# An attention and mixture-of-experts kernel: the row traffic of the expert tiles is issued in another order

## The chip, the cores and the metric

The kernel runs on one core of one Trainium2 chip. The metric is the device time of one execution in microseconds (us). Before the change three executions took 2145.89, 2147.29 and 2153.76 us; the median is 2147.29 us. A further execution, taken with the hardware profiler, is the one whose rows are read below.

## The reference, cut to what matters

```python
B, S, D, d_qk = 8, 2496, 256, 64           # attention
scores = (1 / S) * z @ z.T                 # per batch
x = u * (maximum(scores, 0) ** 2 @ v)      # [B*S, D], N = B*S = 19968 rows

E, F = 8, 1024                             # mixture of experts, one expert a row
logits = x @ w_gate + modality_bias[modality_id]
e_idx  = argmax(logits)                    # the row's expert
gate   = softmax(logits)[e_idx]
out[row] = gate * (maximum(x[row] @ w1[e_idx], 0) @ w2[e_idx])
```

All tensors are float32. Which rows go to which expert is known only when the logits of the last batch are there, so the rows of an expert have to be collected on the chip.

## The kernel before

The first part, some 1240 us, computes the attention of the eight batches, stores each row of x in `row_store` (DRAM) and, batch by batch, routes the rows: a row of `table` (DRAM) is written for each token, at a place that depends on its expert, with the gate's weight, the token's number and the row's place in `row_store`. Nothing of the change lies in its order of work; that is written out by a planner (`pieces`).

The second part runs expert tiles of 512 rows, t = -4 to 35. Tiles -4 to -1 (`EARLY` = 4) hold rows of the expert that had the most rows after seven batches; their rows lie ready when the part begins, and they run while the last batch is still being routed and the other tiles are planned. Tiles 0 to 34 are planned tiles (`UNC` = 35), tile 35 a small one; further ones (`MAXT` = 42) stand behind a branch.

A tile's work on TensorE (`run_tile`) is eight `up` products (f = 0 to 7: six matmuls each) in two groups of four. Behind each group come the `down` products of that group: 16 matmuls with the high parts `hh`, then 8 with the low parts `hl`. ScalarE makes `hh` and VectorE makes `hl` of each `up` product. All engines carry out their instructions in the order in which the program issues them, each engine its own; a DMA is issued by SyncE (SP), or by GpSimd (POOL) where rows are gathered or scattered by an index, and such an issue waits, with all that is queued behind it on that engine, until its data and its buffer are ready.

What is not TensorE's is put into slots. `aside(f)` (L1539) is called at ten places of a tile, f = 0 to 9: behind `up` 0, 1, the whole group and its `down`, the same for the second group (4, 5, 6, 7), and at the end (8, 9). It issues first what lies in the list `put_off` with a slot of at most f, then the next tile's weight quarter number f - 2 (`part_weights_high` on ScalarE, `part_weights_low` on VectorE), then what `between` holds for that slot in the four early tiles, and last the turning of the next tile's rows (`turn_blocks`, `part_high`, `part_low`; slots 5 and 6, in tiles -4 and -3 slots 3 and 4, in the few tiles without `stage` others). In the lines `put(slot, ...)` slots count on through the early tiles: 0 to 7 are tile -4, 8 to 15 tile -3, 16 to 23 tile -2, 24 to 31 tile -1.

The steps that the change moves, each with the engine that issues it:

- `scatter` (L713, POOL): writes 128 tokens' rows of `table`; twelve of them are left for the last batch.
- `plan` (L752, VectorE, five pieces): what each tile holds. Its last piece issues two DMAs on SP: `places` to DRAM, and `meta` from there back to one partition, which waits for the first to land.
- `find(t)` (L859, SP): reads the tile's place from `meta` into a register and loads its rows of `table` as `gate`. The first one waits for all scatters.
- `gather(t)` (L870, POOL): four indirect DMAs that fetch the 512 rows into `got`, by the indices that `find` loaded.
- `keep(t)` (L885, SP): stores `got` to DRAM (`picked`), and waits for the gather to land.
- `fetch(t)` (L892, SP): four DMAs that load `picked` in another arrangement, as `xg`; they wait for the store to land.
- `fetch_weights(t)` (L913, SP): four loads of 512 KB, the expert's weights. They take four of the seven buffers of the tag `x`; `got` takes a fifth.

A tile's result leaves through SP and POOL too. `send(t)` (L1441) at the tile's end: VectorE turns it (`squared`), SP stores it to DRAM (`stage`, four DMAs), in slot 2 of the next tile SP loads it back (`bring`, the tensor `back`), and in slots 4, 5, 6 and 6 ScalarE multiplies a quarter of it by the gate and POOL scatters it to `out` (`put`; in eleven of the tiles as eight DMAs in place of four). ScalarE waits in its own order for `back`, and the `hh` of the second group stand behind that wait. Tiles -2, 33 and 34 have no `stage`; their rows are scattered at once.

In a planned tile t the steps stand in this order before the change, with the slot:

```python
(2) bring of tile t-1, keep(t + 2)
(3) fetch(t + 2), find(t + 3), fetch_weights(t + 2)
(4, 5, 6, 6) put of tile t-1
(7) gather(t + 3)
```

Of the kernel before, what the change touches and what calls it, by code (L numbers as in the profile page):

```python
# [9 lines left out]
F32 = mybir.dt.float32  # L10
# [6 lines left out]
P = 128  # L17
# [5 lines left out]
def ins_of(x):  # L23
    return getattr(x, "ins", x)
# [3 lines left out]
def tile_attention_moe(ctx: ExitStack, tc: tile.TileContext, ut, v, zt, mid, wg, mb, w1, w2, out):  # L28
# [12 lines left out]
    B, S, D = v.shape  # L41
# [5 lines left out]
    J = T // P  # L47
# [5 lines left out]
    XW = 3  # L53
    BLK = 32
    CAP = N
    EARLY = min(4, (B - 1) * S // E // T)
    UNC = -(-N // T) - EARLY
    MAXT = (N + E * (T - 1)) // T - EARLY
# [26 lines left out]
    nq = const.tile([1, 1], I32, name="nq")  # L85
    first = const.tile([1, 2], I32, name="first")
    small = ctx.enter_context(tc.tile_pool(name="small", bufs=1))
    small.tile([P, 16], F32, name="room")


    ph1, feed = ExitStack(), ExitStack()
# [41 lines left out]
    n = NCOL - J  # L133
# [579 lines left out]
    def scatter(b, k):  # L713

        n = 64 if k == NCOL - 1 else P
        i = ins_of(
            nc.gpsimd.indirect_dma_start(  # L717
                out=table,
                out_offset=bass.IndirectOffsetOnAxis(ap=RT[b]["sloti"][:n, k:k + 1], axis=0),
                in_=RT[b]["side"][:n, k, :],  # L720
                in_offset=None,
                bounds_check=E * CAP - 1,
                oob_is_err=False,
            )
        )
        tc.declare_no_dep(i, group="table", reason="each token has a row of its own")
        tc.add_to_no_dep_group("table", i)
        scatters.append(i)
# [23 lines left out]
    def plan():  # L752
# [36 lines left out]
        for n, (x, op, at_least) in enumerate(((is_last, ALU.is_gt, UNC), (least, ALU.is_equal, UNC + 1))):  # L789
            k = odd[:, n:n + 1]  # L790
# [39 lines left out]
        nc.vector.tensor_copy(out=placei, in_=place)  # L830

        nc.sync.dma_start(out=places, in_=placei[0:MAXT])
        nc.sync.dma_start(out=meta, in_=places.rearrange("(o m) n -> o m n", o=1))


# [9 lines left out]
    def wait_rows(i, n):  # L845
        assert len(scatters) >= n
        for s in scatters[ready["n"]:n]:
            tc.add_manual_dep(i, s.name, data, reason="rows of tokens")
        ready["n"] = n
# [4 lines left out]
    SIDE, GOT, KEPT = {}, {}, {}  # L854

    def order_of_rows(t):
        return "(p j) c -> p j c" if is_staged(t) else "(j p) c -> p j c"

    def find(t, r0=0, nj=J):  # L859

        cell = first[0:1, 1:2] if t < 0 else meta[0:1, t, 0:1]
        row = nc.sync.value_load(cell, min_val=0, max_val=(E - 1) * CAP if t < 0 else E * CAP - T)
        side = small.tile([P, J, XW], F32, tag="gate", bufs=6, name="gate")[:, 0:nj, :]
        r0 += (t + EARLY) * T if t < 0 else 0
        src = table[bass.ds(row + r0 if r0 else row, nj * P), :]
        i = ins_of(nc.sync.dma_start(out=side, in_=src.rearrange(order_of_rows(t), j=nj)))
        wait_rows(i, (B - 1 if t < 0 else B) * NCOL)
        SIDE[t] = side

    def gather(t):  # L870
        side = SIDE[t]
        nj = side.shape[1]
        stored_rows = (B - 1 if t < 0 else B) * NCH * T
        GOT[t] = x = rows.tile([P, J, D], F32, tag="x", bufs=NX, name="got")[:, 0:nj]
        for j in range(nj):
            nc.gpsimd.indirect_dma_start(  # L876
                out=x[:, j, :],
                out_offset=None,
                in_=row_store[0:stored_rows],
                in_offset=bass.IndirectOffsetOnAxis(ap=side[:, j, 2:3].bitcast(I32), axis=0),  # L880
                bounds_check=stored_rows - 1,
                oob_is_err=False,
            )

    def keep(t):  # L885
        x = GOT.pop(t)
        nj = x.shape[1]
        n = t + EARLY
        KEPT[t] = to = early_rows[n * T:(n + 1) * T] if t < 0 else picked[t % len(picked)][0:nj * P]
        nc.sync.dma_start(out=to.rearrange(order_of_rows(t), j=nj), in_=x)  # L890

    def fetch(t):  # L892

        src = KEPT.pop(t)
        nt = src.shape[0]
        k = fetched["n"] % 2
        fetched["n"] += 1
        xg = head[k].tile([P, T // BLK, KD * BLK], F32, tag=f"xg{k}", name="xg")[:, 0:nt // BLK, :]
        for b in range(P // BLK):
            cols = slice(b * KD * BLK, (b + 1) * KD * BLK)  # L900
            nc.sync.dma_start(out=xg[b * BLK:(b + 1) * BLK], in_=src[:, cols].rearrange("(t i) c -> i t c", i=BLK))
        TL[t] = (SIDE.pop(t), xg)
# [10 lines left out]
    def fetch_weights(t, some=range(KD + 2)):  # L913

        cell = first[0:1, 0:1] if t < 0 else meta[0:1, t, 1:2]
        e = nc.sync.value_load(cell, min_val=0, max_val=E - 1)
        n = KF // 2
        for q in some:
            if t < 0 and q < KD:
                x = bulk.tile([P, J * D], F32, tag=("vh", "vl")[q], bufs=6, name="wq")  # L920
            else:
                x = rows.tile([P, J * D], F32, tag="x", bufs=NX, name="wq")
            if q < KD:
                mine = w1[bass.ds(e, 1), :, q, :].rearrange("o p f -> (o p) f")
            else:
                mine = w2[bass.ds(e, 1), :, (q - KD) * n:(q - KD + 1) * n, :].rearrange("o p j d -> (o p) (j d)")
            nc.sync.dma_start(out=x, in_=mine)
            fresh_weights[t, q] = x
# [71 lines left out]
    def piece(on, us, need, f, *args, after=(), take=(), drop=(), gate=-1):  # L1000
# [4 lines left out]
    room = {  # L1005
        "s": 1, "bank": 6, "a": NA, "ah": DEPTH, "al": DEPTH, "turn": 2, "zm": ZM, "vh": 6, "vl": 6,
        "zr": 3, "vr": 3, "x": NX, "u": 1,
    }
# [190 lines left out]
    n = last0 + NI + 9  # L1199
    chosen, ready_rows = done_once["choice"], []  # L1200
    for t in range(-EARLY, 0):
        p = transfer(0.5, n + 4, find, t, after=[(chosen, 2.0)] + [(x, 2.5) for x in scattered[:(B - 1) * NCOL]])
        own = Hold("x")
        p = piece("G", 5.2, n + 5, gather, t, after=[(p, 2.0)], take=[own])
        p = transfer(1.6, n + 8, keep, t, after=[(p, 2.5)])
        later.append((p, own))
        ready_rows.append((p, 2.0))
        n += 3
# [13 lines left out]
    with tc.manual_schedule(engines={ET.PE, ET.Activation, ET.DVE, ET.Pool, ET.SP}):  # L1222
# [33 lines left out]
        def ready_at(p):  # L1256
            t = 0.0
            for d, lag in p.after:
                if d.start is None:
                    return None  # L1260
                t = max(t, d.end + lag)
            return t
# [16 lines left out]
        while left:  # L1279
# [6 lines left out]
            for p in lists[e][:80]:  # L1286
                t = ready_at(p)
# [151 lines left out]
    put_off = []  # L1439
# [37 lines left out]
        put_off.append((2, bring))  # L1477
        put_off.extend((min(4 + j, 6), lambda j=j: put(j)) for j in range(J))

    def prefetch(t):  # L1480

        for n in range(t + 1, min(t + 3, UNC + 1)):
            if n in KEPT:
                fetch(n)

    def quarter_tile(t, part, kept=None):

        _, xh, xl = TL[t]
# [126 lines left out]
    def put(slot, *pieces):  # L1615
        n, f = slots[slot]
        between[n][f] += pieces
# [3 lines left out]
    for slot, pieces in ((6, (route_logits, route_exp)), (7, (route_places,)), (8, (route_gates,)), (9, (route_count,)), (10, (route_slots,))):  # L1621
        put(slot, *(lambda p=p: p(B - 1, LATE) for p in pieces))
    for n, k in enumerate(range(LATE.start, NCOL)):
        put(11 + n * 5 // 6, lambda k=k: scatter(B - 1, k))
    planning = plan()
    for slot in (12, 13, 14, 15, 16):
        put(slot, lambda: next(planning, None))
    put(22, lambda: find(0), lambda: find(1), lambda: fetch_weights(0))
    put(23, lambda: gather(0))
    put(24, lambda: gather(1))  # L1630
    put(25, lambda: keep(0), lambda: find(2))
    put(26, lambda: keep(1))
    put(27, lambda: prefetch(-1), lambda: fetch_weights(1))
    put(28, lambda: gather(2))

    ph2.enter_context(tc.manual_schedule(engines={ET.PE, ET.Activation, ET.DVE, ET.Pool, ET.SP}))
    kept = []
    picks = UNC + (MAXT > UNC)

    def order_loads(t):  # L1640
        prefetch(t)
        if t >= 0 and t + 3 < picks:
            find(t + 3, 0, J if t + 3 < UNC else 1)
        if t >= 0 and t + 2 < min(UNC + 1, MAXT):
            fetch_weights(t + 2)

    for t in range(-EARLY, UNC):
        if t == 0:
            assert next(planning, planning) is planning
        if 0 <= t:  # L1650
            if t + 2 < picks:
                put_off.append((2, lambda t=t: keep(t + 2)))
            put_off.append((3, lambda t=t: order_loads(t)))
            if t + 3 < picks:
                put_off.append((7, lambda t=t: gather(t + 3)))
        else:
            order_loads(t)
        if t == UNC - 1 and MAXT > UNC:
            last = quarter_tile(UNC, "a", kept)
            run_tile(t, True, between.get(t + EARLY, {}), beside=last, kept=kept)  # L1660
        else:
            run_tile(t, t + 1 < min(UNC + 1, MAXT), between.get(t + EARLY, {}))
# [73 lines left out]
```

## Time and profile before

| | |
|---|---|
| median of three executions | 2147.29 us (2145.89 to 2153.76) |
| profiled execution | 2151.02 us |
| its span, first to last instruction | 2149.2 us |
| mean granted TensorE clock | 0.994 |
| TensorE busy | 2106.7 us, 98% |
| VectorE busy | 1634.6 us, 76% |
| ScalarE busy | 1423.4 us, 66% |
| GpSimd busy | 617.9 us, 29% |
| DMA packets' share of 16 engines, SP's queue | 69.1% |
| the same, POOL's queue | 5.7% |

TensorE is PE in the rows, its weight loads are PEld, VectorE is DVE, ScalarE ACT, GpSimd POOL, SyncE SP; a q behind the name (SPq) is the engine's sequencer, which issues DMAs. A row of the timeline holds the start in us from the span's start, the length in us, engine, line, operation, what is written and read, and the number of instructions merged into the row; in square brackets, where the engine stood idle before it, for how long and what ended it. The length of a DMA's row is the issue alone, not the transfer.

### The profile page before, as it was taken

The numbers are of one execution on the slowest core, as the hardware profiler recorded it, in microseconds if no ns is written. First come the engines' busy times: TensorE is split into PE (matmuls) and PEld (weight loads), VectorE is DVE, ScalarE is ACT, GpSimd is POOL, SyncE is SP. The second block draws the span as 40 slices with busy tenths as digits, with TensorE's granted clock in tenths as the row PEclk, the third lists the DMA queues.
The fourth block names the chain that finished last, engine by engine and source line by source line (L and its number), as shares of the span: only waits on it lengthen the run. The fifth ranks groups of instructions, "written<-read, shape, count | busy, mean of one in ns | idle before, by whom it ended". The sixth has DMA issues, their size and how long they took to land. (4 is left out here: it accounts for less than half of the span.)

```text
span 2149.2 us, 44097 instructions
## 1 busy us (share of the span) xinstructions
PE 2106.7 (98%) x16614; PEld 1768.8 (82%) x16614; DVE 1634.6 (76%) x2256; ACT 1423.4 (66%) x2011; POOL 617.9 (29%) x544
## 2 busy tenths in 40 slices
PE   9999999999999999999999998999999999999997
PEld 7888988888888888899998787887877877878786
DVE  8889888988899899899899774665566655655664
ACT  8779788778788788788788633454444544544444
POOL 0000400500401303204005515355444445455332
PEclk9999999999999999999999999999999999999999
DMA  7886868867967968968877836778778777777782
GB/s 191 235 247 165 257 199 215 243 185 204 275 165 201 289 159 213 279 159 240 237 176 191 264 69 188 223 222 247 222 226 243 227 239 229 229 238 223 227 243 88
DMA packets 573050, 460.43 MB, mean 214 GB/s; under 512 B 290010, under 2 KB 473946, under 8 KB 572826
## 3 DMA queue, kind: packets, MB, share of 16 engines
q1 hardware_dynamic: 551930, 416.08, 69.1%
q0 software_dynamic: 20896, 41.43, 5.7%
q8 instruction: 132, 2.16, 0.4%
q14 instruction: 92, 0.75, 0.1%
HBM read 283.27 MB, written 174.09 MB: 213 GB/s over the span
## 5 line engine op out<-in xcount | busy, mean ns | idle before, releaser
L493 PE MATMUL acc<-ah,vh 64*128 64x512 f32 (+1 forms) x3120 | 448.3, 384 | 3.0 <-ACT x L548 2.0
L467 DVE TENSOR_TENSOR al<-r,ah 128x1024 fp32r<-128x1024 f32 (+4 forms) x514 | 430.6, 869 | 17.5 <-ACT ah L457 14.7
L493 PE MATMUL acc<-al,vh 64*128 64x512 f32 (+1 forms) x3120 | 438.2, 382 | 5.6 <-DVE al L467 5.6
L493 PE MATMUL acc<-ah,vl 64*128 64x512 f32 (+1 forms) x3120 | 435.8, 382 | 0.0
L1358 ACT ACTIVATE hh<-ph 128x512 fp32r<-128x512 f32 x312 | 182.2, 597 | 376.6 <-PE ph L1354 376.5
L717 POOL DMA_INDIRECT table<-side,sloti x160 | 216.7, 1355 | 651.9 <-DVE side L709 550.8
L1359 DVE SCALAR_TENSOR_TENSOR hl<-ph,hh 128x512 fp32r<-128x512 f32 x312 | 209.9, 684 | 253.7 <-ACT hh L1358 253.4
L1354 PE MATMUL ph<-xh,w 128*128 128x512 f32 x1248 | 398.5, 390 | 0.0
L457 ACT CAST ah<-r 128x1024 fp32r<-128x1024 f32 (+3 forms) x504 | 359.7, 755 | 42.2 <-PE acc L493 29.1
L493 PEld LDWEIGHTS acc<-al,vh 64*128 64x128 f32 x3120 | 308.6, 184 | 52.4 <-DVE al L467 7.8
L493 PEld LDWEIGHTS acc<-ah,vh 64*128 64x128 f32 x3120 | 304.4, 185 | 49.3 <-ACT x L548 2.6
L493 PEld LDWEIGHTS acc<-ah,vl 64*128 64x128 f32 x3120 | 302.3, 184 | 47.1
L1434 PE MATMUL po<-hh,w 128*128 128x512 f32 x1152 | 281.0, 394 | 11.8 <-ACT hh L1358 11.7
L357 ACT ACTIVATE r<-s 128x1024 f32<-128x1024 f32 (+2 forms) x206 | 208.4, 1013 | 123.3 <-PE s L344 121.9
L1354 PEld LDWEIGHTS ph<-xh,w 128*128 128x128 f32 x1248 | 234.6, 188 | 49.2 <-PE acc L493 0.3
L1434 PEld LDWEIGHTS po<-hh,w 128*128 128x128 f32 x1152 | 216.6, 189 | 64.2 <-ACT hh L1358 19.8
L1354 PE MATMUL ph<-xl,w 128*128 128x512 f32 x624 | 243.2, 390 | 0.8 <-DVE xl L974 0.8
L945 DVE TENSOR_TENSOR w<-wq,w 128x1024 fp32r<-128x1024 f32 x148 | 178.2, 1224 | 75.4 <-ACT w L941 75.1
L399 DVE STREAM_TRANSPOSE turn<-r 128x1024 f32<-128x1024 f32 x158 | 195.0, 1237 | 49.1 <-DMA squares<-turn 31.1
L433 ACT ACTIVATE r<-r 128x1024 f32<-128x1024 f32 (+2 forms) x205 | 215.8, 1053 | 4.7
L876 POOL DMA_INDIRECT got<-row_store,gate x157 | 175.6, 1118 | 78.1 <-issue 42.8
L344 PE MATMUL s<-zm 64*128 64x512 f32 (+3 forms) x1452 | 195.8, 373 | 2.0 <-ACT r L357 2.0
(174 smaller groups left out, 2122.8 us busy)
## 6 DMA issues: line engine op xcount, KB each, us to landing
squares<-turn SPq DMA_DIRECT2D x632, 128.0 KB
r<-squares SPq DMA_DIRECT2D x158, 512.0 KB
wq<-in_moe_w_dram SPq DMA_DIRECT2D x148, 512.0 KB
ut<-in_ut_dram SPq DMA_DIRECT2D x40, 512.0 KB
row_store<-x SPq DMA_DIRECT2D x160, 128.0 KB
stage<-squared SPq DMA_DIRECT2D x144, 128.0 KB
back<-stage SPq DMA_DIRECT2D x36, 512.0 KB
picked<-got SPq DMA_DIRECT2D x35, 512.0 KB
```

The lines of the kernel that those rows point to most:

```text
L344: nc.tensor.matmul(out=s[t][:, w], lhsT=lhs, rhs=mv[halves[t], ql, w], start=n == 0, stop=n == 2)
L357: nc.scalar.activation(out=r[:, t, w], in_=s[t][:, w] if g < 2 else s[:, :, w], func=AF.Relu, scale=INV)
L399: nc.vector.transpose(out=turned_to, in_=x)
L433: nc.scalar.square(out=a[:, t, w], in_=r[:, t, w])
L457: copy(out=y, in_=x)
L467: nc.vector.tensor_tensor(out=y, in0=x, in1=h.bitcast(F32), op=ALU.subtract)
L493: nc.tensor.matmul(out=acc[b, c][r][dh][:, :w], lhsT=V[b, k // J][y][halves[r], k % J, dh * P:(dh + 1) * P], rhs=x[halves[r], t, :w], star ...
L717: nc.gpsimd.indirect_dma_start(out=table, out_offset=bass.IndirectOffsetOnAxis(ap=RT[b]["sloti"][:n, k:k + 1], axis=0), in_=RT[b]["side"][ ...
L1354: nc.tensor.matmul(out=ph, lhsT=lhs, rhs=rhs[:, k, :], start=n == 0, stop=n == 3 * KD - 1)
L1358: nc.scalar.activation(out=hh, in_=ph, func=AF.Relu)
L1359: nc.vector.scalar_tensor_tensor(out=hl, in0=ph, scalar=0.0, in1=hh.bitcast(F32), op0=ALU.max, op1=ALU.subtract)
L1434: nc.tensor.matmul(out=po[k], lhsT=w[:, f, q, k * P:(k + 1) * P], rhs=h[f][part], start=f == q == part == 0, stop=f == KF - 1 and part == 1,)
```

## The change

Five things are changed, all in the second part. The scatters of the last batch go two to a slot from slot 11 (to slot 16, not 20). The plan's pieces go into slots 11, 12, 12, 13, 13 and, the DMA of `meta` alone, 15. The finds, gathers, stores and loads of tiles 0 to 3 are ordered anew in the early tiles. In a planned tile, `gather(t + 3)` stands in slot 0, `fetch(t + 2)` in slot 2, `find(t + 4)` and `fetch_weights(t + 2)` in slot 3, `keep(t + 3)` in slot 5, so that the store is issued a tile before its load. The buffers of `gate` become eight, and an unused tile grows by 128 bytes a partition.

```diff
-    small.tile([P, 16], F32, name="room")
+    small.tile([P, 48], F32, name="room")
...
         nc.sync.dma_start(out=places, in_=placei[0:MAXT])
+        yield
         nc.sync.dma_start(out=meta, in_=places.rearrange("(o m) n -> o m n", o=1))
...
-        side = small.tile([P, J, XW], F32, tag="gate", bufs=6, name="gate")[:, 0:nj, :]
+        side = small.tile([P, J, XW], F32, tag="gate", bufs=8, name="gate")[:, 0:nj, :]
...
-    def prefetch(t):
-
-        for n in range(t + 1, min(t + 3, UNC + 1)):
-            if n in KEPT:
-                fetch(n)
...
     for n, k in enumerate(range(LATE.start, NCOL)):
-        put(11 + n * 5 // 6, lambda k=k: scatter(B - 1, k))
+        put(11 + n // 2, lambda k=k: scatter(B - 1, k))
     planning = plan()
-    for slot in (12, 13, 14, 15, 16):
+    for slot in (11, 12, 12, 13, 13, 15):
         put(slot, lambda: next(planning, None))
-    put(22, lambda: find(0), lambda: find(1), lambda: fetch_weights(0))
-    put(23, lambda: gather(0))
-    put(24, lambda: gather(1))
-    put(25, lambda: keep(0), lambda: find(2))
-    put(26, lambda: keep(1))
-    put(27, lambda: prefetch(-1), lambda: fetch_weights(1))
-    put(28, lambda: gather(2))
+    put(18, lambda: find(0), lambda: find(1), lambda: find(2))
+    put(19, lambda: gather(0), lambda: gather(1))
+    put(21, lambda: keep(0))
+    put(22, lambda: fetch_weights(0))
+    put(23, lambda: keep(1), lambda: gather(2))
+    put(24, lambda: fetch(0))
+    put(26, lambda: keep(2), lambda: fetch(1))
+    put(27, lambda: find(3), lambda: fetch_weights(1))
...
-    def order_loads(t):
-        prefetch(t)
-        if t >= 0 and t + 3 < picks:
-            find(t + 3, 0, J if t + 3 < UNC else 1)
-        if t >= 0 and t + 2 < min(UNC + 1, MAXT):
-            fetch_weights(t + 2)
+    def order(t):
+        loads = [
+            (0, t + 3 < picks, lambda: gather(t + 3)),
+            (2, t + 2 < picks, lambda: fetch(t + 2)),
+            (3, t + 4 < picks, lambda: find(t + 4, 0, J if t + 4 < UNC else 1)),
+            (3, t + 2 < min(UNC + 1, MAXT), lambda: fetch_weights(t + 2)),
+            (5, t + 3 < picks, lambda: keep(t + 3)),
+        ]
+        put_off.extend((slot, f) for slot, needed, f in loads if needed)
...
         if 0 <= t:
-            if t + 2 < picks:
-                put_off.append((2, lambda t=t: keep(t + 2)))
-            put_off.append((3, lambda t=t: order_loads(t)))
-            if t + 3 < picks:
-                put_off.append((7, lambda t=t: gather(t + 3)))
-        else:
-            order_loads(t)
+            order(t)
+        elif t == -EARLY:
+            fetch(1 - EARLY)
+            fetch(2 - EARLY)
+        elif t < -2:
+            fetch(t + 2)
```

## Rows read from the trace of the kernel before

**Rows 1.** Timeline of PE: first matmuls of tiles 1, 2 and 33.

```profile
1361.38 0.39 PE L1354 MATMUL ph<-xh,w 128*128 128x512 f32 x1
...
1383.14 0.39 PE L1354 MATMUL ph<-xh,w 128*128 128x512 f32 x1
...
2085.59 0.39 PE L1354 MATMUL ph<-xh,w 128*128 128x512 f32 x1
```

**Rows 2.** Waits of ACT in the second part: total us, times, longest.

```profile
ACT back L1468 <- DMA back<-stage: 39.5, 24, 4.4
```

**Rows 3.** Timeline of SP, tiles 4 and 5.

```profile
1428.09 2.75 SPq L1450 DMA_DIRECT2D stage<-squared  x4
1435.41 0.34 SPq L1462 DMA_DIRECT2D back<-stage  x1
1440.25 0.34 SPq L890 DMA_DIRECT2D picked<-got  x1
...
1449.13 2.07 SPq L927 DMA_DIRECT2D wq<-in_moe_w_dram  x4
1451.29 5.15 SPq L1450 DMA_DIRECT2D stage<-squared  x4
1461.05 0.34 SPq L1462 DMA_DIRECT2D back<-stage  x1
```

**Rows 4.** Timeline of ACT: first product with `back` in tiles 0 and 5.

```profile
1352.55 0.50 ACT L1468 ACTIVATE back<-back,gate 128x256 f32<-128x256 f32 x1
...
1465.30 0.51 ACT L1468 ACTIVATE back<-back,gate 128x256 f32<-128x256 f32 x1 [3.52 <-DMA back<-stage]
```

**Rows 5.** Timeline of SP, tiles -2 to 0.

```profile
1306.06 1.73 SPq L866 DMA_DIRECT2D gate<-table  x2
...
1318.92 0.33 SPq L890 DMA_DIRECT2D picked<-got  x1
...
1333.94 2.10 SPq L927 DMA_DIRECT2D wq<-in_moe_w_dram  x4
1340.07 2.37 SPq L1450 DMA_DIRECT2D stage<-squared  x4
1345.61 0.34 SPq L1462 DMA_DIRECT2D back<-stage  x1
```

**Rows 6.** Timeline of PE: ends of tiles -3 and -1, and tile 10.

```profile
1286.11 1.98 PE L1434 MATMUL po<-hl,w 128*128 128x512 f32 x8
...
1329.89 0.61 PE L1434 MATMUL po<-hl,w 128*128 128x512 f32 x2
1336.19 3.10 PE L1434 MATMUL po<-hl,w 128*128 128x512 f32 x6 [5.69 <-DVE hl L1359]
...
1581.98 4.88 PE L1434 MATMUL po<-hh,w 128*128 128x512 f32 x12 [1.94 <-ACT hh L1358]
```

**Rows 7.** Timeline of DVE: the plan's pieces in tiles -3 and -2, and tile -1.

```profile
1279.85 0.23 DVE L755 TENSOR_TENSOR p_cnt<-base,base 128x8 f32<-128x8 f32 x1
...
1281.55 1.22 DVE L974 TENSOR_TENSOR xl<-xt,xh 128x1024 fp32r<-128x1024 f32 x1
...
1284.32 1.28 DVE L1359 SCALAR_TENSOR_TENSOR hl<-ph,hh 128x512 fp32r<-128x512 f32 x2
1285.52 0.15 DVE L786 SCALAR_TENSOR_TENSOR p_least<-p_up 128x8 f32<-128x8 f32 x1
...
1288.62 1.30 DVE L1446 STREAM_TRANSPOSE squared<-po 128x512 f32<-128x512 f32 x2
...
1290.72 0.20 DVE L820 TENSOR_SCALAR p_place<-part,p_picked 128x1 f32<-128x1 f32 x1
...
1292.38 1.28 DVE L1359 SCALAR_TENSOR_TENSOR hl<-ph,hh 128x512 fp32r<-128x512 f32 x2
...
1334.31 1.25 DVE L962 STREAM_TRANSPOSE xt<-xg 128x1024 f32<-128x1024 f32 x1 [7.41 <-DMA xg<-picked]
```

**Rows 8.** Timeline of POOL: the put ahead of the last scatter.

```profile
1302.52 0.97 POOL L1383 DMA_INDIRECT out_dram<-back,gate  x1 [6.12 <-ACT back L1468]
```

## The prediction

> **What bounds the kernel now.** I read the busy shares first: TensorE is at 98%, so nothing but its own idle or slow time can be won, and the question is how much of that there is. The view of waits puts a few us down to PE in the second part, but it counts only what is left when the modelled end of the last matmul is past. The starts of tiles tell it exactly. Tiles 1 and 2 start 21.76 us apart [rows 1], and no planned tile takes less: that is 96 matmuls of 0.2267 us. From tile 1's start to tile 33's there are 32 tiles, 724.21 us for 32 x 21.76 = 696.32. So 27.9 us are lost there, a little in each of some twenty tiles.
>
> Where they go, the waits of ScalarE say: 24 times, 39.5 us in all, it stood before its first product with `back`, up to 4.4 us [rows 2], and the `hh` of the second group stand behind that. The reader should follow one such tile on SP [rows 3]. In tile 4 `keep` could go only at 1440.25, when the gather had landed; the load of what it stored, the find and the weights followed, the weights 8.88 us later at 1449.13; the stores of `stage`, which belong at the tile's boundary, came behind them at 1451.29, with 2 MB just ahead of them. Their issue took 5.15 us where 2.75 us is usual, and `back` went 9.76 us after the first of them. It landed 4.24 us after that, at 1465.30, 3.52 us after ScalarE was free for it [rows 4]. Against this stands tile 0 [rows 5]: the weights went 6.13 us ahead of `stage`, `back` 5.54 us behind it, and ScalarE, which came to it at 1352.55, 12.48 us behind `stage`, did not wait [rows 4]. In tile 4 itself, with the gather under way, it was 7.32 us [rows 3]. So the lead of the weights over `stage` decides whether `back` is late. Some waits cost more than themselves, as TensorE runs slower after them: behind one of 1.94 us twelve matmuls took 4.88 us [rows 6], where 11 x 0.2267 + 0.39 = 2.88 is usual.
>
> The second loss is one stall ahead of tile 0. TensorE stands 5.69 us in tile -1 [rows 6] because VectorE waited 7.41 us for the rows of tile 0 [rows 7], and its next six matmuls take 3.10 us where 1.52 is usual. Undisturbed, eight matmuls after 1329.89 tile 0 would begin at 1331.70 and tile 1 at 1353.46; it begins at 1361.38 [rows 1], so this costs 7.9 us.
>
> **The planned tiles.** No instruction is added or taken away; SP and POOL issue the same DMAs in another order. On POOL nothing moves: a gather in slot 0 of tile t stands between the same puts as one in slot 7 of tile t-1, though it now serves a tile further ahead. On SP the order becomes bring, four fetches, find, weights, `keep`. The fetches load what was stored a tile ago and wait for nothing. Even if all of the 8.88 us between `keep` and weights [rows 3] stayed, the weights would go 7.32 + 8.88 = 16.2 us behind `stage` at the latest, so 5.6 us or more ahead of the next; most likely ten. That is the lead of tile 0, and `back` would come 5.54 to 7.32 us behind `stage` and be there 4.24 us later, at 9.8 to 11.6, before ScalarE's 12.48. The loss of 27.9 us goes. Its bounds are nothing gained (the bytes are the same) and all of it; tile 0's row is nearest, and I leave 2.0 us for single tiles.
>
> The added wait is `keep` in slot 5. Behind it on SP stand the four stores of `stage` and the next bring, and ScalarE waits for those. Its gather landed 12.16 us behind `stage` in tile 4, where a put of eight DMAs had held POOL, and the next `stage` came 23.2 us behind the first [rows 3]: 11 us of cover, cost nothing. The weights also need buffers that VectorE frees in slots 2 and 3; if SP stands there, only `keep` waits, in the same cover. The cost with the cover gone is a rival below.
>
> **The early tiles.** The last scatter stood behind a put for which POOL waited 6.12 us [rows 8]. Ahead of it, all twelve are out 6.12 + 0.97 = 7.1 us sooner, and the finds that wait for them go at 1299.0, not 1306.06 [rows 5]. From there to the turning of tile 0's rows it took 1334.31 - 1306.06 = 28.25 us [rows 5, 7]. Were that way no shorter, the rows would be there at 1327.2, and VectorE was free for them at 1334.31 - 7.41 = 1326.9, or 1.9 us later by the next paragraph. It is shorter, as `fetch(0)` no longer waits for a store just issued, nor stands behind a find. So the 7.9 us go; the bounds are 0 and 7.9.
>
> SP's queue there: the weights of tile 0 now stand behind `keep(0)`, which came 12.86 us after its find [rows 5], so at 1311.9 at the latest, up to 5.9 us later than now; their first use moves 1.9 us. That costs between nothing and 4.0 us; as `keep(0)` no longer shares the DMA engines with those weights, I take nothing. `meta` goes ahead of a `stage`, but `places` lands sooner too: nothing either way. POOL's gathers of tiles 0 and 1 now stand ahead of the four puts of tile -3; nothing reads those.
>
> The plan's pieces cost something. Pieces 3 and 4 (1285.52 to 1288.62, 3.10 us) and 5 (1290.72 to 1292.38, 1.66 us) now come ahead of `hl` of f = 6, piece 1 (1279.85 to 1281.55, 1.70 us) no longer does, in a stretch that VectorE fills without a gap. That `hl` moves from 1284.32 [rows 7] to 1287.4 and is done at 1288.0, that of f = 7 at 1288.7. TensorE wants them 2 and 3 matmuls after 1286.11 [rows 6], at 1286.6 and 1286.8. So it stalls 1.9 us, a new wait of PE on `hl` at the end of tile -3. Bounds: nothing, and 3.9 if TensorE runs slower after it, by the 2.0 us that tile 10 lost so [rows 6]. I take 1.9.
>
> The Trainium skill (TensorE: Matmul & The Clock Gate, "What's actually happening") lets the clock fall only for a window of inactivity, and by that such a stall between running matmuls would cost 1.9 us alone. Tile 10's row disagrees, with slow matmuls after 1.94 us of waiting; by it the sum would be 2 us higher.
>
> The larger `gate` and the padding are no instructions. They shift addresses, which no row shows; I take nothing.
>
> **The sum**, against the profiled execution's 2151.0 us: 2151.0 - 27.9 + 2.0 - 7.9 + 1.9 = 2119.1. The median of the runs shown, 2147.3, is 3.7 us lower. What is left when the losses are gone should be the same for both, so the forecast is 2119 us, and its own range 2112 to 2131.
>
> **The rivals.**
>
> A: the load only moves. 2 MB of weights then run beside the puts and the `keep`, and if these engines are as full as at the boundary now, `stage` and `back` stay as late as they are. Only the early tiles gain, 7.9 - 1.9 = 6.0: 2141 us from the median. For it speaks that no byte is saved; against it, that tile 0 and tile 5 differ by the lead of the weights alone. The Trainium skill (DMA: Bandwidth & Descriptors, "Issuing engines are not separate DMA queues") states that all DMAs run on the same 16 engines and interleave, whoever issues them; that is the ground of this rival.
>
> B: tile 0's rows are late again, or its weights are (the 4.0 us above and slow matmuls after it), and only the planned tiles gain: 2119 + 7.9 = 2127. For it speaks that `keep(0)` and `keep(1)` both wait on SP for gathers; against it the 7 us of lead.
>
> C, on the other side: SP stands at `keep` for the gather, with `stage` behind it. It decides from a gather that lands later than the next boundary, 11 us later than in tile 4. In the eleven tiles behind a put of eight DMAs, `stage` 5 us late would put `back` 3.7 us beyond ScalarE, 41 us in all: 2119 + 41 = 2160. Nothing in the trace comes near that.
>
> D: the early finds and the order on SP change nothing that ends last, because `stage` is slow by itself: 2147. Against it stands tile 0's 5.54.
>
> **How the numbers follow.** Forecast 0.70, A 0.11, B 0.09, C 0.06, D 0.04. The smallest difference that can be told here is 0.5%, 10.7 us, so faster means below 2136.6: the forecast and B, 0.79. Same takes A and D, 0.15; slower is C, 0.06. The range of 2112 to 2142 reaches to A and leaves out C, D, part of A and the forecast's lower end, about 0.2.
>
> **What would show it.** ScalarE's wait for `back` falls from 39.5 us to below 5, and the 32 tiles from 724.2 to below 701. On SP the weights go eight us or more ahead of `stage`, `back` 5.5 to 7.3 behind it. The stall of 5.69 us is gone, and one of PE on `hl` of some 1.9 us stands at the end of tile -3. A `keep` that SP waits for beyond a tile's boundary, or a `back` over 10 us behind `stage` with the weights far ahead, would make the forecast wrong.

## The result, and the profile after

The changed kernel took 2119.74 us (median of four runs, 2117.06 to 2120.79), the kernel before 2149.2 us beside it (2145.89 to 2153.76). The ratio is 0.986, with a 95% interval of 0.9837 to 0.9882: faster by 1.4%. Times and ratios below leave out four executions in a slower state (2309.90 us in 6, 7476.14 in 11, 3001.81 and 3016.16 of the kernel before beside 12).

The profiled execution of the changed kernel took 2120.79 us. Its page gives the same picture as before, TensorE without a gap worth naming:

```profile
span 2119.0 us, 44055 instructions
...
PE 2093.4 (99%) x16614; PEld 1834.6 (87%) x16614; DVE 1640.6 (77%) x2256; ACT 1421.3 (67%) x2011; POOL 614.1 (29%) x544
```

So the starts of tiles tell where the 30.2 us between the two profiled executions (2151.0 and 2120.8) came from. These are the first matmuls of tiles -3 to 0 in the timeline of PE, before (start in us, duration; those of tiles 1 and 33 are in [rows 1]):

```profile
1265.93 0.39 PE L1354 MATMUL ph<-xh,w 128*128 128x512 f32 x1
...
1287.93 0.39 PE L1354 MATMUL ph<-xh,w 128*128 128x512 f32 x1
...
1309.91 0.40 PE L1354 MATMUL ph<-xh,w 128*128 128x512 f32 x1
...
1339.09 0.63 PE L1354 MATMUL ph<-xh,w 128*128 128x512 f32 x1
```

and of tiles -3 to 1 and of tile 33, after:

```profile
1265.76 0.39 PE L1355 MATMUL ph<-xh,w 128*128 128x512 f32 x1
...
1289.90 0.60 PE L1355 MATMUL ph<-xh,w 128*128 128x512 f32 x1
...
1313.54 0.40 PE L1355 MATMUL ph<-xh,w 128*128 128x512 f32 x1
...
1335.33 0.39 PE L1355 MATMUL ph<-xh,w 128*128 128x512 f32 x1
...
1359.97 0.39 PE L1355 MATMUL ph<-xh,w 128*128 128x512 f32 x1
...
2056.29 0.39 PE L1355 MATMUL ph<-xh,w 128*128 128x512 f32 x1
```

Differences of such starts, for both kernels, give this account:

| stretch | before, us | after, us | change |
|---|---|---|---|
| start to tile -3 | 1265.93 | 1265.76 | -0.2 |
| tile -3 | 22.00 | 24.14 | +2.1 |
| tile -2 | 21.99 | 23.64 | +1.7 |
| tile -1 | 29.17 | 21.79 | -7.4 |
| tile 0 | 22.29 | 24.64 | +2.4 |
| tiles 1 to 32 | 724.21 | 696.32 | -27.9 |
| tile 33 to the end of the span | 63.6 | 62.7 | -0.9 |

The 32 planned tiles take 696.32 us, which is 32 x 21.76 to the last digit: nothing is lost in any of them [rows 1]. The early tiles gain 7.4 us in tile -1 and give back 6.2 in the three others.

Why the planned tiles lose nothing shows in the waits of ScalarE. Of the 24 waits for `back` [rows 2] one is left (total us, times, longest), and that one is in tile 0:

```profile
ACT back L1469 <- DMA back<-stage: 3.4, 1, 3.4
```

and in SP's timeline of tiles 4 and 5, to be read against [rows 3]:

```profile
1426.19 2.39 SPq L1451 DMA_DIRECT2D stage<-squared  x4
1431.46 0.34 SPq L1463 DMA_DIRECT2D back<-stage  x1
...
1437.28 2.01 SPq L928 DMA_DIRECT2D wq<-in_moe_w_dram  x4
1441.53 0.33 SPq L891 DMA_DIRECT2D picked<-got  x1
1447.95 2.26 SPq L1451 DMA_DIRECT2D stage<-squared  x4
1453.16 0.34 SPq L1463 DMA_DIRECT2D back<-stage  x1
```

The weights go 10.67 us ahead of `stage` (1447.95 - 1437.28), where it was 2.16; the issue of `stage` takes 2.26 us, not 5.15; `back` goes 5.21 us behind it, not 9.76. This lead, from the first of the four loads of weights to the first store of `stage` behind them, has a median over tiles 1 to 32 of 11.47 us (before 3.93); the median distance from `stage` to `back` is 5.23 us (before 8.55). `keep` now ends SP's list, 6.42 us ahead of the next `stage`.

The new loss of tiles -3 and -2 is a wait where there was none [rows 6]. In the timeline of PE at the end of tile -3, after:

```profile
1285.96 0.61 PE L1435 MATMUL po<-hl,w 128*128 128x512 f32 x2
1288.04 2.04 PE L1435 MATMUL po<-hl,w 128*128 128x512 f32 x6 [1.47 <-DVE hl L1360]
1289.90 0.60 PE L1355 MATMUL ph<-xh,w 128*128 128x512 f32 x1
```

Six matmuls behind it take 2.04 us where 1.52 is usual, as the second goes 0.60 us behind the first: the next `hl` is done only at 1288.58. The view of windows (us, busy time and count of PE, PEld, DVE, ACT and POOL, granted clock, DMA share, GB/s) has the granted clock at 1.00, which is 2.4 GHz, up to the start of tile -2, and then at 0.50, 1.2 GHz, from 1289.91 to 1293.32:

```profile
1284.00:1288.04 4.04, 2.57 (x13) 1.80 (x11) 3.55 (x19) 0.00 (x0) 3.13 (x4) 1.00 0.11 33
1288.04:1289.91 1.87, 1.77 (x7) 1.24 (x8) 1.26 (x2) 0.00 (x0) 1.26 (x3) 1.00 0.03 1
1289.91:1293.32 3.41, 3.41 (x10) 2.67 (x9) 0.73 (x2) 0.60 (x1) 2.69 (x3) 0.50 0.54 146
```

So the 2.1 us of tile -3 are lost at the full clock, nearly all in waiting for `hl`, and the 1.7 us of tile -2 are lost by matmuls at half the clock, half of that stretch.

The loss of tile 0 is the old fault in a new place. In SP's timeline of tiles -1 and 0, after, the weights of tile 1 stand behind a `keep` that waits for a gather, and so 2.18 us ahead of `stage`, where they had 6.13 us before [rows 5]:

```profile
1329.68 0.34 SPq L891 DMA_DIRECT2D picked<-got  x1
...
1334.94 2.07 SPq L928 DMA_DIRECT2D wq<-in_moe_w_dram  x4
1337.12 3.85 SPq L1451 DMA_DIRECT2D stage<-squared  x4
1346.82 0.34 SPq L1463 DMA_DIRECT2D back<-stage  x1
```

`back` goes 9.70 us behind `stage`, and ScalarE, which did not wait for it in tile 0 before [rows 4], now does:

```profile
1351.80 0.51 ACT L1469 ACTIVATE back<-back,gate 128x256 f32<-128x256 f32 x1 [3.43 <-DMA back<-stage]
```

### The profile page after: what moved, and what is told of

Read it like the earlier page. It is cut to its first block, busy times and chain, and to the rows that moved or that the text cites. A ratio compares the mean times of both kernels' runs of the same rounds, so it can differ in the third digit from the quotient of the medians.

```text
span 2119.0 us, 44055 instructions
## 1 busy us (share of the span) xinstructions
PE 2093.4 (99%) x16614; PEld 1834.6 (87%) x16614; DVE 1640.6 (77%) x2256; ACT 1421.3 (67%) x2011; POOL 614.1 (29%) x544
## 3 DMA queue, kind: packets, MB, share of 16 engines
q8 instruction: 132, 2.16, 0.4%
## 5 line engine op out<-in xcount | busy, mean ns | idle before, releaser
L493 PE MATMUL acc<-ah,vh 64*128 64x512 f32 (+1 forms) x3120 | 454.7, 384 | 3.5 <-ACT ah L457 1.5
L493 PE MATMUL acc<-al,vh 64*128 64x512 f32 (+1 forms) x3120 | 444.4, 382 | 4.2 <-DVE al L467 4.2
L493 PE MATMUL acc<-ah,vl 64*128 64x512 f32 (+1 forms) x3120 | 442.9, 382 | 0.0
L493 PEld LDWEIGHTS acc<-al,vh 64*128 64x128 f32 x3120 | 327.7, 184 | 32.6 <-DVE al L467 6.3
L493 PEld LDWEIGHTS acc<-ah,vh 64*128 64x128 f32 x3120 | 322.7, 185 | 31.9 <-ACT x L548 2.1
L493 PEld LDWEIGHTS acc<-ah,vl 64*128 64x128 f32 x3120 | 322.1, 185 | 27.8
L1435 PE MATMUL po<-hh,w 128*128 128x512 f32 x1152 | 273.4, 389 | 1.7 <-ACT hh L1359 1.7
```

The source lines that it names most:

```text
L493: nc.tensor.matmul(out=acc[b, c][r][dh][:, :w], lhsT=V[b, k // J][y][halves[r], k % J, dh * P:(dh + 1) * P], rhs=x[halves[r], t, :w], star ...
L1435: nc.tensor.matmul(out=po[k], lhsT=w[:, f, q, k * P:(k + 1) * P], rhs=h[f][part], start=f == q == part == 0, stop=f == KF - 1 and part == 1,)
```

## The experiments

The theory was the prediction's: what costs the planned tiles their 27.9 us is the 2 MB of weights issued just ahead of `stage` on SP's queue. Its first rival was that the gain is that of the early tiles, or of the gather and store that now come a tile ahead of the load. The period of tiles 1 to 32 ("planned tiles" below, "tiles 1 to 33" in the expectations: from the start of tile 1 to that of tile 33) is the measure wherever a total is too blunt; the undisturbed value is 696.32 us.

**1. Planned order alone.** The changed kernel with the early tiles, the last scatters and the plan's pieces of the kernel before (its first lines below; `keep(2)` and `find(3)` placed so that tile 0 has what it needs).

```
-    put(18, lambda: find(0), lambda: find(1), lambda: find(2))
-    put(19, lambda: gather(0), lambda: gather(1))
...
+    put(22, lambda: find(0), lambda: find(1), lambda: fetch_weights(0))
+    put(23, lambda: gather(0))
+    put(24, lambda: gather(1))
...
+    put(28, lambda: gather(2), lambda: find(3))
```

> The planned tiles in the new order, the early tiles as before the change (find(3) and keep(2) are added where the two orders meet). Theory (the lead of the weights over stage decides when back comes): tiles 1 to 33 take 696 to 699 us where they took 724.2 before, the stall of 5.7 us ahead of tile 0 stays, there is no new stall on hl in tile -3; 2122 to 2125 us. Rival (it is the early start of the finds and gathers that sets the planned tiles apart): less than half of the 27.9 us comes, so over 2135 us.

Measured: 2123.76 us against 2148.65 for the kernel before, ratio 0.988 (0.9864 to 0.9897). The planned tiles take 696.32 us; the stall ahead of tile 0 is still there (tile -1 takes 29.10 us). So the planned order brings the 27.9 us by itself.

**2. Early order alone.** The changed kernel with the planned tiles ordered as before.

```
-            (2, t + 2 < picks, lambda: fetch(t + 2)),
...
-            (3, t + 2 < min(UNC + 1, MAXT), lambda: fetch_weights(t + 2)),
-            (5, t + 3 < picks, lambda: keep(t + 3)),
...
+                put_off.append((2, lambda t=t: keep(t + 2)))
+            put_off.append((3, lambda t=t: order_loads(t)))
```

> The early tiles in the new order, the planned tiles as before the change. Theory: tiles 1 to 33 lose their 25 to 31 us as before (720 to 728 us), ScalarE waits some 40 us for back; the early tiles gain the 7.9 us stall and lose 3.9 in tile -3; tile 0 has no weights just ahead of its stage at another time than now, so up to 2.9 more; 2145 to 2149 us. Rival (the early start carries the gain): under 2135 us.

Measured: 2148.01 us, ratio 0.9994 (0.9978 to 1.0009): no difference that can be told. The planned tiles take 724.92 us, the median lead is 3.99 us, and the waits of ScalarE are those of [rows 2]:

```profile
ACT back L1469 <- DMA back<-stage: 39.4, 21, 4.0
```

From tile -3 to tile 1 it takes 91.73 us, 3.7 less than before; this part is real in the profile and too small for the total.

**3 and 4. The weights issued late.** If the lead is the cause, putting it back must bring the loss back with everything else as changed. The changed kernel issues the weights last, in slot 7, and makes them wait: in 3 for ScalarE's last product with `back`, in 4 for VectorE's `xl`, which is later.

```
+            for s in behind:
+                tc.add_manual_dep(i, s.name, data, reason="weights late")
...
-            (3, t + 2 < min(UNC + 1, MAXT), lambda: fetch_weights(t + 2)),
...
+            (7, t + 2 < min(UNC + 1, MAXT), lambda: fetch_weights(t + 2, behind=scaled)),
```

> The changed kernel, but the weights are issued last of a tile and made to wait for ScalarE's last product with back (slot 6). Theory: the weights go some 3.8 us ahead of stage, and by the rows of before at that lead back comes 7.3 to 8.9 us behind stage, so ScalarE waits 0 to 1.4 us in a tile and PE loses 0 to 0.9: tiles 1 to 33 take 700 to 720 us; 2124 to 2144 us. Rival (the load and store a tile apart carry the gain, wherever the weights stand): 696 to 698 us for the tiles, 2118 to 2122 us.

> The same, but the weights wait for the low part of the next tile's rows (VectorE, slot 6, some 21 us into a tile). Theory: they go about 2 us ahead of stage, as in the worst tiles of before, where back came 9.8 to 11.9 us behind stage and PE lost 2.3 to 4.9 us: with most of 32 tiles so, tiles 1 to 33 take 750 to 850 us; 2180 to 2270 us. Rival (the load and store a tile apart carry the gain): 696 to 700 us for the tiles, 2118 to 2124 us.

Measured: 3 took 2130.02 us, ratio 0.9914 (0.9898 to 0.9931), and 4 took 2225.25 us, ratio 1.0358 (1.0341 to 1.0376), the kernel before being 2148.65 beside them. SP's timeline of one tile in 3:

```profile
1729.10 2.05 SPq L928 DMA_DIRECT2D wq<-in_moe_w_dram  x4
...
1733.80 4.39 SPq L1455 DMA_DIRECT2D stage<-squared  x4
...
1743.01 0.34 SPq L1467 DMA_DIRECT2D back<-stage  x1
```

and in 4:

```profile
1736.30 2.05 SPq L928 DMA_DIRECT2D wq<-in_moe_w_dram  x4
1738.46 4.43 SPq L1455 DMA_DIRECT2D stage<-squared  x4
...
1747.89 0.34 SPq L1467 DMA_DIRECT2D back<-stage  x1
```

The waits of ScalarE for `back`, in 3:

```profile
ACT back L1473 <- DMA back<-stage: 15.6, 17, 1.8
```

and in 4:

```profile
ACT back L1473 <- DMA back<-stage: 111.4, 34, 4.8
```

Both came out in the range expected of the theory. Medians over the 32 tiles:

| | lead of the weights, us | `back` behind `stage`, us | planned tiles, us |
|---|---|---|---|
| changed | 11.47 | 5.23 | 696.32 |
| 3 | 4.39 | 7.51 | 703.28 |
| before | 3.93 | 8.55 | 724.21 |
| 4 | 2.16 | 9.66 | 795.68 |

The later the weights, the later `back`, and the loss grows steeply once `back` comes later than ScalarE has room for. The medians hide the spread: in 3 every lead lies between 4.20 and 4.70 us, before they run from 2.16 to 5.15, and the nine planned tiles with a lead of 2.16 to 3.08 us hold 23.0 of the 27.9 us lost.

Two other ways in which late weights could cost time can be read off the traces. The load itself does not come too late: in 4 ScalarE casts the first quarter of the weights 6.28 us behind their issue (1742.58 - 1736.30), and none of its 130 casts (L944) has idle time ahead of it. And SP, standing for the weights, also issues `stage` later, 2.04 us (median) into the tile, where it is 0.94 in the changed kernel; that is a part of the lateness in 4, but in 5 below `stage` goes 2.48 us into the tile and nothing is lost.

**5. The weights first, nothing else.** The kernel before, with find and weights of a tile issued ahead of `keep` and of the fetches; store and load of rows stay in one tile.

```
     def order_loads(t):
-        prefetch(t)
...
             fetch_weights(t + 2)
+        if t >= 0 and t + 2 < picks:
+            keep(t + 2)
+        prefetch(t)
...
-            if t + 2 < picks:
-                put_off.append((2, lambda t=t: keep(t + 2)))
```

> The kernel before with one thing moved: in a planned tile the find and the weights are issued ahead of keep and fetch, which stay a pair in one tile, with their round trip. Theory (only the weights' lead over stage counts): the weights go 10 us or more ahead of stage, tiles 1 to 33 take 696 to 700 us, the stall ahead of tile 0 stays; 2120 to 2126 us. Rival (the store has to be a tile ahead of its load, or SP stands at it when stage is due): 705 us or more for the tiles, over 2130 us.

Measured: 2121.69 us against 2148.56, ratio 0.9873 (0.9857 to 0.989); the planned tiles take 696.32 us. In SP's timeline of tiles 4 and 5 the load of rows that waits for its store now stands just ahead of `stage`, and `back` still goes 6.15 us behind it:

```profile
1435.03 2.03 SPq L927 DMA_DIRECT2D wq<-in_moe_w_dram  x4
1441.53 0.33 SPq L890 DMA_DIRECT2D picked<-got  x1
1446.66 1.93 SPq L901 DMA_DIRECT2D xg<-picked  x4
1448.69 3.12 SPq L1450 DMA_DIRECT2D stage<-squared  x4
1454.84 0.34 SPq L1462 DMA_DIRECT2D back<-stage  x1
```

So the tile between store and load is not needed: moving the weights is enough. Tile -1 takes 29.12 us here, as in 1.

**6. `keep` first.** The changed kernel with `keep(t + 3)` in slot 2, ahead of the fetch and the weights, so that the weights wait behind a gather again.

```
+            (2, t + 3 < picks, lambda: keep(t + 3)),
             (2, t + 2 < picks, lambda: fetch(t + 2)),
...
-            (5, t + 3 < picks, lambda: keep(t + 3)),
```

> The changed kernel with keep(t+3) moved from slot 5 to slot 2, ahead of the fetches and the weights, so that SP again stands for the gather before the weights go. Theory: in the tiles behind a put of eight DMAs keep goes some 12 us behind stage and the weights 4 to 6 us ahead of the next one, elsewhere 8 to 10; by the rows of before back then comes 5.5 to 8.5 us behind stage, so tiles 1 to 33 take 696 to 704 us; 2119 to 2128 us. Rival (waiting on SP for the gather is what cost the time): 710 us or more, over 2132 us.

Measured: 2119.66 us, ratio 0.9867 (0.9847 to 0.9887), planned tiles 697.02 us. The median lead is 8.11 us but falls to 4.48 in some tiles; only tiles 10 and 22 lose more than 0.02 us, with 22.11 and 22.08. The gather is issued in the same tile as its `keep` (slots 0 and 2), and `keep` does hold the weights up. The waits of SP in the second part, before:

```profile
SPq L901 <- DMA picked<-got: 136.0, 34, 4.8
...
SPq L890 <- DMA got<-row_store,gate: 57.3, 13, 8.1
```

and in 6:

```profile
SPq L891 <- DMA got<-row_store,gate: 84.3, 21, 6.6
```

SP stands longer for gathers than before the change. What is gone is the other wait ahead of the weights, that of the four loads for the store just issued, 34 times and 136.0 us: the loads now fetch what was stored a tile ago. From `keep` to the weights it takes 5.69 us (median), not 8.86. So with the weights behind `keep` the tile between store and load pays, and with the weights first (5) it is not needed.

**7. The plan spread out.** The changed kernel with the plan's pieces spread so that no more of them than before come ahead of `hl` of f = 6.

```
-    for slot in (11, 12, 12, 13, 13, 15):
+    for slot in (11, 11, 12, 14, 15, 15):
```

> The changed kernel with the plan's pieces in slots 11, 11, 12, 14, 15, 15. Both theories: the stall of PE on hl in tile -3 is gone, so tile -1 starts 3.9 us sooner after tile -3. Theory (in the early tiles SP's queue ends last: stage of tile -1 stands behind the weights of tile 1, these behind keep(2), that waits for gather(2) on POOL): tile 0 waits longer for back by about as much, tile 1 starts no more than 1 us sooner; 2118 to 2121 us. Rival (the stall is worth what it takes): 2115 to 2117 us.

Measured: 2122.66 us, ratio 0.9886 (0.9865 to 0.9908). Tiles -3 and -2 take 22.01 and 21.99 us, so all 3.8 us that they lost go with the wait for `hl`. From tile -3 to tile 1 only 0.3 us of it is kept (93.89 us for 94.21). Tile -1 takes 23.01 us, as VectorE waits for the rows of tile 0 again, and tile 0 takes 26.89, for its wait for `back` is longer, ScalarE having come to it sooner, and the granted clock is 0.50 (1.2 GHz) from 1353.46 to 1356.87, behind the waits that follow from it on TensorE:

```profile
1328.48 1.25 DVE L963 STREAM_TRANSPOSE xt<-xg 128x1024 f32<-128x1024 f32 x1 [2.17 <-DMA xg<-picked]
```

```profile
1350.19 0.51 ACT L1469 ACTIVATE back<-back,gate 128x256 f32<-128x256 f32 x1 [4.89 <-DMA back<-stage]
```

The total lies above what either side expected; the four executions took 2118.62 to 2127.51 us.

**8. Weights of tile 1 sooner.** The changed kernel with the weights of tile 1 ahead of `keep(2)`.

```
-    put(26, lambda: keep(2), lambda: fetch(1))
-    put(27, lambda: find(3), lambda: fetch_weights(1))
+    put(26, lambda: find(3), lambda: fetch_weights(1), lambda: fetch(1))
+    put(27, lambda: keep(2))
```

> The changed kernel with find(3) and the weights of tile 1 issued in slot 26 ahead of fetch(1), and keep(2) in slot 27 behind them. Theory: the weights of tile 1 go 8 us or more ahead of the stage of tile -1, ScalarE's wait of 3.4 us for back in tile 0 is gone, tile 0 takes 21.8 to 22.2 us where it took 24.6; the stall in tile -3 stays; 2115.5 to 2118 us. Rival (keep(2) and fetch(1) come late in their place, or back is late for its own sake): tile 0 or 1 still over 23.5 us, 2119 us or more.

Measured: 2120.99 us, ratio 0.9868 (0.9852 to 0.9885). The part aimed at came out: the weights go 10.64 us ahead of `stage`, `back` 7.11 behind it, and tile 0 takes 21.78 us, not 24.64.

```profile
1331.37 2.07 SPq L928 DMA_DIRECT2D wq<-in_moe_w_dram  x4
...
1342.01 3.31 SPq L1451 DMA_DIRECT2D stage<-squared  x4
1349.12 0.34 SPq L1463 DMA_DIRECT2D back<-stage  x1
```

The total expected of it, 2115.5 to 2118, did not come; it lies where the rival's was put, without the rival's cause. In this profiled run tile -3 starts 4.6 us later than in the changed kernel's, in a part of the program that the edit does not touch, and that hides 2.9 us.

**9 and 12. Both early losses taken away.** The edits of 7 and 8 together, in two runs; **10** is the changed kernel again beside 9. What was expected of 9, 10 and 12, in this order:

> The changed kernel with both edits of the early tiles: the plan's pieces spread (slots 11, 11, 12, 14, 15, 15) and the weights of tile 1 ahead of keep(2). Theory (the two hide each other: one puts the stall in tile -3, the other keeps it in tile 0): from the start of tile -3 to that of tile 1 it takes 87.3 to 88.5 us (four tiles of 21.76, tile -2 at 21.99) where the changed kernel took 94.2; 2112 to 2116 us, some 6 us below the changed kernel beside it. Rival (the gathers on POOL set the early tiles whatever SP does): 91 us or more, 2117 us or more.

> The changed kernel once more on the same chip, to compare the others of this job with: 2117 to 2122 us, 94 us from tile -3 to tile 1, 696.3 us for tiles 1 to 33.

> The kernel of e9_both_early once more, since in its job every kernel, the one before too, ran 55 to 65 us longer, with waits of PE that the profile puts to issue. Theory: 87.3 to 88.5 us from tile -3 to tile 1, tiles 1 to 33 in 696.3 us, 2112 to 2116 us beside a kernel before of 2147 to 2150. Rival (the gathers on POOL set the early tiles): 91 us or more, 2117 us or more.

Measured: 9 took 2180.69 us (ratio 0.9879, 0.9835 to 0.9923), 10 took 2183.1 (0.9864, 0.9826 to 0.9902), and 12 took 2184.9 (0.9894, 0.9861 to 0.9926), while the kernel before took 2207.87 (beside 9 and 10) and 2206.28 (beside 12). In these runs and in 11 every kernel took some 60 us longer, most of it ahead of the tiles, some in tiles -2 and -1. A part is time in which PE waited for nothing that the profile shows ("issue"); in 10 its waits begin:

```profile
PE acc L493 <- issue: 11.4, 26, 0.9
PE po L1435 <- issue: 8.5, 1, 8.5
PE po L601 <- issue: 7.8, 17, 0.5
```

In 9 tiles -3 and 0 take 22.01 and 21.76 us, and in 12 the same: the wait for `hl` and that for `back` are gone from them. But tile 0 takes 21.76 in 10 as well, where tile -1 takes 33.93 us and SP has the time that it lacks otherwise. The totals of 9 and 10 differ by 2.4 us, inside their spread. From tile -3 to tile 1 it takes 106.13 us in 9 and 106.67 in 12, where 87.3 to 88.5 were expected, and 104.70 in 10: tiles -2 and -1 take 30.88 and 31.48 us in 9, with waits of PE put to issue (6.1 us the longest) and of ScalarE put to what the profile calls remote (14.8 us), which the trace of the changed kernel does not have there. So the gain of some 6 us expected of both edits together is not shown, and stays open; the rows of tile 0, for which VectorE waits in 7, would limit it. The planned tiles take 696.32 us in 9 and 12, 696.34 in 10: their gain does not depend on that delay.

**11. The small padding.** The changed kernel with `room` as before, so that the two larger `gate` buffers alone shift what lies behind them.

```
-    small.tile([P, 48], F32, name="room")
+    small.tile([P, 16], F32, name="room")
```

> The changed kernel with the unused tile at 64 bytes a partition, as before the change, so that all later tiles lie 128 bytes lower. The prediction took nothing for the addresses: within 2 us of the changed kernel, no tile longer. Rival (the padding was part of the gain): 2125 us or more, with the loss in the first part, ahead of tile -3.

Measured: 2194.30 us, ratio 0.9933 (0.9899 to 0.9966), where 10 took 2183.1. Neither side was right: the loss is there, but in the planned tiles. They take 705.81 us in the profiled execution, 9.5 more than in 10: the odd ones 22.31 us, the even ones 21.80, all the way through, and PE has no wait in them. The view of windows for tiles 2 and 3 (columns as above):

```profile
1443.19:1464.99 21.80, 21.80 (x98) 18.02 (x97) 13.81 (x16) 10.87 (x17) 6.75 (x7) 1.00 0.91 235
1464.99:1487.30 22.31, 22.31 (x97) 18.08 (x96) 13.95 (x19) 10.91 (x17) 10.52 (x9) 1.00 0.88 227
```

and for tiles 1 and 2 of 10, the changed kernel, beside which 11 is to be read:

```profile
1430.13:1451.89 21.76, 21.76 (x97) 18.02 (x96) 13.82 (x17) 10.87 (x17) 8.45 (x9) 1.00 0.91 241
1451.89:1473.65 21.76, 21.76 (x97) 18.02 (x96) 13.81 (x17) 10.87 (x17) 6.87 (x8) 1.00 0.87 237
```

The clock is 1.00 in all four, and the 96 matmuls of tile 3 are simply slower, 22.31 / 96 = 0.2324 us for 0.2267. So 128 bytes of padding a partition decide over 9.5 us. Which buffer's address does it was not tried.

## Why the prediction was right

The forecast of 2119 us stands against 2119.74. The main mechanism was right; that the total is so close is in part luck, as the early tiles show. Step by step:

- **The planned tiles** were sized right and for the right reason. The lead was said to be "most likely ten" us and is 11.47; `back` 5.5 to 7.3 us behind `stage`, and is 5.23. Runs 1 to 5 show that it is the lead: restoring it alone is enough (5), and shortening it brings 7.0 us of loss in 3 and 99.4 in 4. The 2.0 us left for single tiles were not needed.
- **The wait of `keep`** cost nothing, as put. In the second part SP waits for gathers 15 times, 42.2 us in all, where it was 13 times and 57.3; none reaches a boundary, as `keep` goes 5.83 us or more ahead of the next `stage` in every planned tile. Rival C is out.
- **The stall ahead of tile 0** is gone: tile -1 takes 21.79 us, 7.4 less, where 7.9 was said (the other 0.5 was tile 0's share of it). But the way from the finds to the rows of tile 0 did not get shorter than 28.25 us, as was argued: in 7, where VectorE stands for the rows, they come 28.60 us behind the finds (1328.48 - 1299.88), and tile -1 loses 1.2 us. In the changed kernel the loss of tiles -3 and -2 hides that, which is luck. The weights of tile 0 go at 1310.67, inside the bound of 1311.9, and cost nothing (before they went at 1308.70, so the bound was 3.2 us later, not 5.9).
- **The plan's pieces** were placed right and priced low. `hl` of f = 6 moves to 1287.30, worked out as 1287.4, and TensorE waits for it where it was said. But the term was 1.9 us and measured 3.8, near the upper bound of 3.9: the stall itself is 2.1 us in tile -3, and 1.7 more are lost in tile -2 at the granted clock of 0.50, as behind tile 10's wait [rows 6], where it is 0.50 from 1582.46 to 1585.87. Run 7 takes both parts away at once. By the Trainium skill (TensorE: Matmul & The Clock Gate, "What's actually happening"), whose clock falls only for a window of inactivity, 1.9 us would have been all; these rows disagree, as PE had waited 1.47 us and was busy before and behind that.
- **Tile 0** is the step that was not there. The sum placed the weights of tiles 0 and t + 2, and not those of tile 1, which stand behind `keep(2)`; the rule that the prediction itself found, that the lead decides, would have told it: 2.18 us of lead, and 2.9 us lost (24.64 - 21.76). Run 8 shows that by moving them (with the find) ahead of `keep(2)`.
- **The padding and the larger `gate`** were taken as nothing. For both together that holds, but 11 shows that the buffers without the padding would have cost 9.5 us: right by the whole edit, not by its working.

The sum said -31.9 us from the profiled execution and -30.2 came. The early tiles were to give 6.0 and gave 1.2; of these 4.8 us too little, 3.1 were covered by the 2.0 left for single tiles, 0.9 at the end and 0.2 at the start. So the total is closer than its terms. Of the rivals, A and D fall to runs 1 to 5, B's time (2127) to the total, though the weights late at an early tile that it spoke of are what happened, one tile on.

No version was shown to be faster than the changed one: 5, 6 and 8 (2121.69, 2119.66 and 2120.99 us) cannot be told from it.

## What to carry to other kernels

Where a small store and its reload must be back by a fixed time, look at what large transfer stands just ahead of them on the same queue, and at what *that* waits for: here a 2 MB load, held up behind a wait for a gather and one for a store, cost 28 us over 32 tiles by lying 2 to 5 us ahead of a store instead of 11. Issue the large transfer ahead of the waits (5), or take the longest of the waits away by letting a load fetch what was stored a tile ago (6); either was enough here. Then apply the rule to every place where the pattern occurs, the ramp into the loop included: here tile 0 had it again.

## What was not expected of the hardware

In run 11, at a granted clock of 1.00 and with no wait in sight, matmuls of the same shape took 0.2324 us in the odd tiles and 0.2271 in the even ones (22.31 and 21.80 / 96), only because buffers lay 128 bytes a partition lower; in 10 it is 0.2267 in both.

And the same kernel took 2119.74 us in one set of runs and 2183.1 in another. The two profiled executions, 2120.79 and 2190.93 us, are 70.1 us apart, and 59.7 of these were lost before tile -3 (1325.43 - 1265.76), with waits for issue and granted clocks of 0.97 to 0.98 in the stretches from 200 to 1000 us, 1.00 in the first set. Why is open: runs 1 to 4, 5 to 8, 9 to 11 and 12 were on four different chips, so the chip is not excluded. The planned tiles took the same 696.3 us in both: a small difference in the tiles is to be read from the tiles, not from the total.
